# Gate and up of 256-query chunks: one copy out of PSUM and a multiplication on GpSimd, in a program ordered by a planner with other assumed step times

## The chip, the cores and the metric

The kernel runs on one core of one Trainium2 chip. The metric is the device time of one launch in microseconds (us), as the median of several runs. Five engines work side by side, each through its own list of instructions in a fixed order: TensorE (PE; PEld is its weight load), VectorE (DVE), ScalarE (ACT), GpSimd (POOL), and SyncE (SP), which here only issues DMAs. They wait for one another through semaphores. SBUF is the on-chip memory, PSUM the eight banks into which TensorE writes.

## The reference

One transformer block with 2048 tokens, width 640, 32 heads of width 20 and a bilinear feed-forward part of width 1536, all in bfloat16:

```python
mod = (silu(c) @ w_mod)                       # six vectors: sa, ca, ga, sb, cb, gb
h = layernorm(x) * (1 + ca) + sa
q, k, v = split(h @ wqkv)                     # 32 heads, 20 wide
p = softmax(q @ k.T / sqrt(20))               # 32 x 2048 x 2048
x = x + ga * ((p @ v) @ wo)
h = layernorm(x) * (1 + cb) + sb
x = x + gb * (((h @ w_gate) * (h @ w_up)) @ w_down)
```

## The kernel before

**Tiling.** The 2048 queries are cut into seven chunks, one of 512 and six of 256. For each chunk the heads are taken in eight sets of four. One pair of chunk and set is an item. TensorE writes an item's scores (L1524) into PSUM in units of 128x512, transposed, keys on the partitions (in a 256-query chunk two key tiles side by side). Then there are two ways to the exponential. ScalarE takes two units at once, 128x1024, with its own function (L1561, tile PP). Or VectorE approximates it: it adds a bias and turns the score into an int16 (L1585, tile DB, "P1"), masks it into two tiles (L1617 and L1625, tile DSS, for four units at once, a "quad"), and the first of these is multiplied with DB, on GpSimd in four pieces of 512 (L1637) or on VectorE in one piece of 2048 (L1622). The table QUADS says how many quads of each item go VectorE's way. Both kinds are multiplied with the values V on TensorE (L2192) and summed in PSUM. A quad costs TensorE two such products where a ScalarE unit costs one.

**End of an item.** VectorE transposes the sum (L1717), takes a reciprocal (L1723), GpSimd or VectorE normalizes (L1725), VectorE transposes back (L1734), and DMAs (L1746) put the rows into the tile Ocp.

**Around it.** In chunk 0 the projections of K, Q and V are still being made, spread between the scores (L1230, L970). Most of K and Q is written to DRAM (k_rows, q_rows; L1276) and read back in the layout of the scores (L1289, L1298), all issued by SP. When a chunk's heads are done, its suffix runs between the scores of the next chunk: output projection (L1827), second layernorm (L1844 to L1851), transposition (L1889), then for each of the twelve 128-wide slices of the feed-forward width a gate and an up matmul, and the down projection (tiles wd and hprod, evacuated at L2062). The last chunk's suffix stands alone at the end of the program, the tail.

**Gate and up of a 256-query chunk.** Ten groups of four matmuls fill one PSUM bank: the gate in columns 0 to 255, the up part in columns 256 to 511. Chunks 1 to 5 have twelve such rounds each, sixty in all. Then two VectorE instructions:

```python
f = lambda e: e.tensor_copy(gsb[:, gs, 0:n], ps[:, r.b["b"], 0:n])                                    # L1959
f = lambda e: e.tensor_tensor(hprod[:, fc, 0:n], ps[:, r.b["b"], n:2 * n], gsb[:, gs, 0:n], ALU.mult) # L1966
```

The tile gsb has two halves of 512 columns, used in turn, and the copy of a round waits until the product of two rounds before has been made. PSUM's bank is given back when the second instruction is done.

**What sets the order.** The kernel carries a planner. While the program is built, the class Sched steps through time with an assumed duration for each task, and at each step gives each free engine the ready task with the best priority. What comes out is a fixed list for every engine; on the chip nothing is chosen any more. Among the assumed figures: P1 and other reads of PSUM cost `n * 1.042 + 67` ns, a landing of a DMA is reckoned from its size, tasks that would share an SBUF port between VectorE and GpSimd are kept apart by a lock (LKTOL), and TensorE is fed filler matmuls (L2523) when its recent work falls below a limit (FILL_HARD, HAM_MIN). Scores come first: pick_pe issues the next pair of score units as soon as the PSUM banks for it are free, there are two sets of them, so the scores of a pair need the exponential two before to have been read. d_attach hangs a VectorE unit onto such a score group when a PSUM bank is free. Between scores TensorE gets products with V, projections and suffix rounds. The table STAGE changes some limits of the planner from item to item. The tasks touched by the change are built in `after` in `suffix`, in `packed_round`, in `item_end_tasks`, in `Sched._enable`, `Sched.finish_issue` and `d_attach`.

Of the kernel before, what the change touches and what calls it, by code (L numbers as in the profile page):

```python
# [30 lines left out]
EARLY_M = 900.0  # L31
DMA_M0 = 60000.0
# [3 lines left out]
HAM_MIN = 3100.0  # L36
# [3 lines left out]
class Task:  # L40
    __slots__ = ("head", "hval", "hknow", "eng", "dur", "lat", "deps", "emits", "ctr", "prio", "gate", "acq", "on_start", "slots",
                 "start", "done", "needed", "val", "know", "nleft", "ready", "users", "name", "mode", "seq", "rt", "sem",
                 "nbytes", "cond", "alt", "land", "firm", "lk", "dead", "key")

    def __init__(self, eng, dur, emits, deps=(), ctr=None, prio=0.0, lat=None, gate=0, acq=(), on_start=None,
# [26 lines left out]
        self.firm = False  # L72
        self.lk = 0
# [58 lines left out]
class Sched:  # L132
# [102 lines left out]
    def finish_issue(self, task, start, dur):  # L235
        task.start = start
        if task.nbytes:
# [118 lines left out]
def emit_program(nc, sched, nsem_dma=56):  # L356
# [124 lines left out]
QUADS = ((0, 4, 3, 3, 3, 4, 4, 4), (2, 2, 1, 2, 2, 2, 1, 2), (2, 2, 1, 2, 2, 2, 1, 2), (2, 2, 1, 2, 2, 2, 1, 2), (2, 2, 1, 2, 2, 2, 1, 2), (2, 2, 1, 2, 2, 2, 1, 2), (2, 1, 2, 2, 2, 1, 2, 0))  # L481
# [30 lines left out]
ZFILL = 1  # L512
WD_POOL, WD_PRIO = 1, 400.0
# [31 lines left out]
FILL_HARD = 3600.0  # L545
# [23 lines left out]
    0: {"PVMIN": 2, "HOLD": 95, "PVTOL": 249, "D_RES": 58, "PVCAP": 6, "X_HALF": 0.0, "XDPRIO": 1.343, "FILL_MIN": 3463.3, "LKTOL": 300.0, "EAGER": 9, "PVMAX": 14, "X_LATE": -179.96, "TPRIO": 0.75, "STEAL_GAP": 200, "D_LATE": 16, "PV_KEEP": 2},  # L569
    1: {"PVCAP": 15, "XBACK": 1, "FILL_MIN": 4629.7},  # L570
    2: {"DL": 0.376},
    4: {"HOLD": 58.0, "X_LATE": -39.3},
    5: {"D_LATE": 7, "PVMAX": 3},
    6: {"X_LATE": 168.4, "FILL_MIN": 5225.9, "HOLD": 156.4},
    7: {"DL": 0.501},
    8: {"FILL_MIN": 2868.8},
    10: {"X_HALF": 69.3, "HOLD": 73.7, "PVMAX": 5},
    11: {"DL": 0.443},
    12: {"DL": 0.459, "HOLD": 108.3, "X_LATE": 6.6},
    13: {"DL": 0.417},  # L580
    15: {"X_LATE": 86.8},
    16: {"HOLD": 135.0, "FILL_MIN": 4362.5},
    17: {"X_LATE": -17.4, "LKTOL": 338.9, "HOLD": 52.0},
    19: {"DL": 0.471, "PVMAX": 7, "HOLD": 113.6},
    20: {"DL": 0.391, "PVMAX": 10},
    21: {"X_LATE": -85.4, "PVMIN": 3},
    24: {"DL": 0.464, "STEAL_GAP": 210.6, "X_LATE": -52.5, "PVCAP": 14, "HOLD": 116.4, "LKTOL": 98.1},
    25: {"DL": 0.549, "LKTOL": 370.4, "HOLD": 156.3},
    26: {"DL": 0.411, "PVMIN": 1, "X_LATE": 2.0, "EAGER": 6, "X_HALF": 58.0},
    27: {"DL": 0.473},  # L590
    29: {"HOLD": 148.6, "D_LATE": 5, "LKTOL": 267.5, "D_RES": 36, "PVMAX": 3},
    30: {"EAGER": 11},
    31: {"X_LATE": -99.6, "HOLD": 173.2, "X_HALF": 164.9, "PV_KEEP": 2},
    33: {"DL": 0.442, "PVMIN": 7, "PV_KEEP": 3, "X_HALF": 147.4},
    34: {"PVMIN": 3, "X_HALF": 26.9, "STEAL_GAP": 91.8, "EAGER": 8, "X_LATE": 136.8, "D_RES": 25},
    35: {"X_HALF": 148.7},
    36: {"DL": 0.524},
    37: {"FILL_MIN": 4112.0, "EAGER": 8, "X_LATE": -201.5},
    39: {"STEAL_GAP": 162.9, "EAGER": 9},
    42: {"PVMAX": 8, "FILL_MIN": 4334.4, "PV_KEEP": 3},  # L600
    43: {"HOLD": 127.6},
    46: {"D_LATE": 20, "PV_KEEP": 3, "X_LATE": -80.9},
    53: {"LKTOL": 820.1, "X_HALF": 73.5},
    54: {"PVTOL": 279.6, "FILL_MIN": 4011.5, "X_HALF": 31.3},
# [15 lines left out]
def build_kernel(nc, A_x, A_wqkv, A_wo, B_x, B_w_gate, B_w_up, B_w_down, c, w_mod, out):  # L620
# [603 lines left out]
    def packed_round(kind, b, tc, prio, gate=0, late_q=False):  # L1224
# [69 lines left out]
        else:  # L1294
# [6 lines left out]
            if tc not in LATEQ:  # L1301
                proj_early.append(r.last)
# [1048 lines left out]
    def d_attach(ts, t, pos, rows, limit, relax):  # L2351
        n = 0
        while n < limit:
# [15 lines left out]
            if ga is None or ga[0] > t:  # L2369
                break  # L2370
# [258 lines left out]
```

## Time and profile before

| what | value |
|---|---|
| median of 3 runs | 805.0 us (804.37 to 805.67) |
| the profiled execution's own time | 805.59 us |
| its span from first to last instruction | 803.8 us |
| mean granted TensorE clock | 0.998 |
| PE busy | 790.4 us, 98% |
| ACT busy | 764.8 us, 95% |
| DVE busy | 697.8 us, 87% |
| POOL busy | 386.0 us, 48% |

The profile is of one execution. A row of a group of instructions gives the line, the engine, the operation, what it writes and reads, partitions x elements, the count, then the busy time in us, the mean time of one in ns, and after the second bar the idle time of the engine just before them with what ended it. Instructions of one engine overlap a little at their ends, so the mean of one is longer than the step from one start to the next. TensorE's busy time is modelled: a busy PE isn't a PE at its peak.

### The profile page before, as it was taken

How to read it: one execution, taken by the hardware profiler on the slowest of the kernel's cores; microseconds unless marked ns; L12 is line 12 of the kernel's file. 1: busy time of each engine (PE TensorE's matmuls, PEld its weight loads, DVE VectorE, ACT ScalarE, POOL GpSimd, SP SyncE). 2: the span in 40 equal slices, each digit the busy share in tenths (PEclk: the TensorE clock that was granted, in tenths of full speed). 3: DMA queues.
4: the chain of work that ended last, by engine and by line, in shares of the span. 5: the costliest groups of instructions: out<-in, count | busy, mean ns of one | idle time of the engine just before them, and what ended most of it. 6: DMA issues, size and time to landing. Idle time of an engine off the chain costs nothing.

```text
span 803.8 us, 37761 instructions
## 1 busy us (share of the span) xinstructions
PE 790.4 (98%) x16595; PEld 380.6 (47%) x16595; DVE 697.8 (87%) x1401; ACT 764.8 (95%) x847; POOL 386.0 (48%) x396
## 2 busy tenths in 40 slices
PE   8999999999999999999999999999999999999998
PEld 4433433333244434445555455555555555555567
DVE  7978788799989999988999999999899988898754
ACT  6899899999999999999999999999999999999961
POOL 3347455654366565763444443545534554455300
PEclk9999999999999999999999999999999999999999
DMA  9733212212341532120032404231540254414420
GB/s 297 243 113 91 62 43 64 61 33 76 92 109 50 167 88 52 35 55 13 24 81 65 95 16 112 57 73 39 121 89 15 54 118 94 98 37 106 92 68 18
DMA packets 154314, 64.66 MB, mean 80 GB/s; under 512 B 116951, under 2 KB 154151, under 8 KB 154151
## 3 DMA queue, kind: packets, MB, share of 16 engines
q1 hardware_dynamic: 153223, 61.10, 30.0%
q8 instruction: 132, 2.16, 1.1%
q10 hardware_dynamic: 928, 1.15, 0.5%
q14 instruction: 31, 0.25, 0.1%
HBM read 50.63 MB, written 8.99 MB: 74 GB/s over the span
## 4 chain that ended last, share of the span: by engine, by line
PE 77%; ACT 14%; DVE 5%; issue 2%; DMA 1%; SPq 1%; POOL 0%; DVEq 0%; ACTq 0%
PE ps_all L1524 26%; PE ps_all L970 21%; PE ps_all L2192 19%; ACT PP L1561 14%; PE ps_all L1230 4%; PE ps_all L966 3%; DVE DB L1585 2%; PE ps_all L1889 1%; PE ps_all L1166 1%; PE ps_all L1127 1%; DVE DSS L1617 1%; PE ps_all L2523 0%; DVE DSS L1625 0%; DMA QT<-q_rows 0%; PE ps_all L991 0%
## 5 line engine op out<-in xcount | busy, mean ns | idle before, releaser
L1561 ACT ACTIVATE PP<-ps_all 128x1024 bf16<-128x1024 f32 x810 | 748.5, 1090 | 6.7 <-PE ps_all L1524 4.8
L1637 POOL TENSOR_TENSOR DSS<-DB,DSS 128x512 bf16<-128x512 bf16 x268 | 305.0, 1157 | 290.6 <-DVE DSS L1625 254.2
L1585 DVE TENSOR_SCALAR DB<-ps_all 128x512 int16<-128x512 f32 x428 | 285.5, 681 | 50.5 <-PE ps_all L1524 48.0
L1524 PE MATMUL ps_all<-QT,KT 32*128 32x256 bf16 (+2 forms) x3648 | 319.4, 287 | 4.5 <-DMA QT<-q_rows 0.8
L1524 PEld LDWEIGHTS ps_all<-QT,KT 32*128 32x128 bf16 x3648 | 93.9, 92 | 204.1 <-ACT PP L1561 141.5
L2192 PE MATMUL ps_all<-PP,Vf 128*32 128x256 bf16 (+2 forms) x2892 | 163.6, 291 | 0.5 <-DVE KPB L1242 0.3
L970 PE MATMUL ps_all<-h2T,stg 128*32 128x256 bf16 (+2 forms) x2716 | 122.9, 281 | 0.3 <-DVE DB L1585 0.2
L2192 PEld LDWEIGHTS ps_all<-PP,Vf 128*32 128x32 bf16 (+1 forms) x2892 | 54.5, 94 | 76.4 <-issue 67.6
L2192 PE MATMUL ps_all<-DSS,Vf 128*32 128x256 bf16 (+1 forms) x1512 | 88.7, 291 | 0.0
L1617 DVE TENSOR_SCALAR DSS<-DB 128x2048 int16<-128x2048 int16 x107 | 77.2, 722 | 0.8
L970 PEld LDWEIGHTS ps_all<-h2T,stg 128*32 128x32 bf16 x2716 | 61.6, 96 | 26.9 <-issue 22.0
L1625 DVE TENSOR_SCALAR DSS<-DB 128x2048 int16<-128x2048 int16 x107 | 73.2, 684 | 0.8 <-PE ps_all L2192 0.8
L970 PE MATMUL ps_all<-wd,hprod 128*32 128x320 bf16 (+1 forms) x1404 | 61.0, 277 | 0.0
L1725 POOL TENSOR_TENSOR OTn<-OT,invT 128x256 bf16<-128x256 f32 (+1 forms) x49 | 35.3, 721 | 37.7 <-DVE invT L1723 37.5
L1622 DVE TENSOR_TENSOR DSS<-DB,DSS 128x2048 bf16<-128x2048 bf16 x40 | 51.5, 1287 | 0.0
L2192 PEld LDWEIGHTS ps_all<-DSS,Vf 128*32 128x32 bf16 x1512 | 36.5, 95 | 20.9 <-issue 12.4
L970 PE MATMUL ps_all<-wV,hT 128*32 128x160 bf16 x1280 | 38.9, 236 | 0.9 <-DVE DB L1585 0.3
L970 PEld LDWEIGHTS ps_all<-wd,hprod 128*32 128x32 bf16 x1404 | 31.2, 96 | 14.2 <-issue 10.8
L1717 DVE STREAM_TRANSPOSE OT<-ps_all 128x256 f32<-128x256 f32 (+2 forms) x57 | 27.1, 475 | 8.8 <-PE ps_all L2192 8.5
L1230 PE MATMUL ps_all<-hT,wk 128*32 128x512 bf16 x360 | 32.3, 382 | 0.0
L970 PEld LDWEIGHTS ps_all<-wV,hT 128*32 128x32 bf16 x1280 | 24.6, 97 | 15.9 <-issue 8.2
L1230 PE MATMUL ps_all<-hT,wq 128*32 128x512 bf16 x375 | 31.3, 382 | 0.6 <-DVE OT L1717 0.6
(133 smaller groups left out, 556.1 us busy)
## 6 DMA issues: line engine op xcount, KB each, us to landing
stg<-in_B_w_gate_dram SPq DMA_DIRECT2D x74, 160.0 KB
stg<-in_B_w_up_dram SPq DMA_DIRECT2D x74, 160.0 KB
KT<-k_rows SPq DMA_DIRECT2D x112, 32.0 KB
QT<-q_rows SPq DMA_DIRECT2D x48, 64.0 KB
Ocp<-OcT SPq DMA_DIRECT2D x164, 10.0 KB
wm<-in_w_mod_dram SPq DMA_DIRECT2D x3, 800.0 KB
x<-in_A_x_dram SPq DMA_DIRECT2D x7, 320.0 KB
k_rows<-KPA SPq DMA_DIRECT2D x16, 128.0 KB
```

What stands on the lines that cost most here:

```text
L970: return lambda e, b: e.matmul(ps[32 * x:32 * x + 32, b, c0 + o:c0 + o + w], lhs()[:, 32 * x:32 * x + 32], rhs() if w == n else rhs()[:, o ...
L1230: f = [lambda e, b_, k=k, x=x: e.matmul(ps[x:x + min(32, w - x), b_, :], wx[:, k, r0 + x:r0 + min(x + 32, w)], hT[tc][:, k, :], tile_posit ...
L1524: ems.append(lambda e, i=i, kt=kt: e.matmul(dstf()[:, i * u.n:(i + 1) * u.n], KT[32 * u.s:32 * u.s + 32, u.j, kt * 128:(kt + 1) * 128], QT ...
L1561: return e.activation(PPs[g % 2][:, cellp["p"], 0:nu * 512], ps[:, b0:b0 + nu, :].rearrange("p b c -> p (b c)"), AFT.Exp, scale=ESCALE)
L1585: return e.tensor_scalar(DBl[st_["slot"]][:, x * 512:(x + 1) * 512], bank(cell["b"]), EBIAS, 0.0, op0=ALU.add, op1=ALU.max)
L1617: return e.tensor_scalar(DSl[st_["ss"][0]][:, :], DBl[st_["slot"]][:, :], 0x7F, 0x3F00, op0=ALU.bitwise_and, op1=ALU.bitwise_or)
L1622: return e.tensor_tensor(d, DBl[st_["slot"]][:, :].bitcast(BF16), d, ALU.mult)
L1625: return e.tensor_scalar(DSl[st_["ss"][1]][:, :], DBl[st_["slot"]][:, :], 0x7F80, 2, op0=ALU.bitwise_and, op1=ALU.bitwise_or)
L1637: return e.tensor_tensor(d, DBl[st_["slot"]][:, x * w:x * w + w].bitcast(BF16), d, ALU.mult)
L1717: t1 = Task("dve", n * 1.1 + 70, lambda e: e.transpose(OT[:, 0:n], ps[:, item_info[it]["bank"], 0:n].rearrange("p (b q r) -> p b r q", q=3 ...
L1725: f3 = lambda e: e.tensor_tensor(OTn[:, 0:n].rearrange("p (b c r) -> p b r c", c=32, r=2), OT[:, 0:n].rearrange("p (b r c) -> p b r c", c= ...
L2192: ems.append(lambda e, i=i, kt=kt, stt=stt, stp=stp: e.matmul(ps[32 * s:32 * s + mc, bk, 0:u.n], Vf[:, (kt * H + 4 * u.j + s) * VW:(kt * H ...
```

## The change

For the sixty rounds of gate and up of chunks 1 to 5, one VectorE copy takes all 512 columns out of PSUM, and GpSimd multiplies the two halves within SBUF. The bank is given back by the copy; the half of gsb by the product. Beside it the planner gets other figures, and the table STAGE is another one.

```diff
+                    if GU_POOL and not tail:
+                        f = lambda e: e.tensor_copy(gsb[:, gs, 0:2 * n], ps[:, r.b["b"], 0:2 * n])
+                        fa = lambda e: e.copy(gsb[:, gs, 0:2 * n], ps[:, r.b["b"], 0:2 * n])
+                        f2 = lambda e: e.tensor_tensor(hprod[:, fc, 0:n], gsb[:, gs, n:2 * n], gsb[:, gs, 0:n], ALU.mult)
+                        eg = evac(2 * n, ps_cost(2 * n), f, fa, ds)
+                        r.hp = pool(n * POOL_NS + 180.0, f2, [eg] + (hp_free if alt else bd.get("hp", []) + proj_early + kv_last),
+                                    prio=GU_PRIO)
+                        r.hp.lk = 2
+                        return [eg]
...
-                g_use[gs] = r.evac[1]
-                hp.append(r.evac[1])
+                hpt = r.hp if GU_POOL and not tail else r.evac[1]
+                g_use[gs] = hpt
+                hp.append(hpt)
```

The planner's figures: writes of late Q rows land 900 ns later than assumed so far (QW_M), reads of Q rows 1500 ns later (QR_M); P1 starts 28 ns later after its scores (P1_X); a VectorE unit is hung onto scores only where the PSUM bank was given back by VectorE 110 ns earlier (SD_X); transposes, reciprocal and one evacuation of VectorE get other durations; two limits for filler go up; one quad fewer in chunk 1.

```diff
+QW_M, QR_M = 900.0, 1500.0
+P1_X, SD_X = 28.0, 110.0
-HAM_MIN = 3100.0
+HAM_MIN = 3150.0
...
-            t = max(t, d.done + SEM)
+            t = max(t, d.done + SEM + (P1_X if task.name[:2] == "P1" and d.mode == "S" else 0.0))
...
+            task.done += task.xm
...
-QUADS = ((0, 4, 3, 3, 3, 4, 4, 4), (2, 2, 1, 2, 2, 2, 1, 2), (2, 2, 1, 2, 2, 2, 1, 2), (2, 2, 1, 2, 2, 2, 1, 2), (2, 2, 1, 2, 2, 2, 1, 2), (2, 2, 1, 2, 2, 2, 1, 2), (2, 1, 2, 2, 2, 1, 2, 0))
+QUADS = ((0, 4, 3, 3, 3, 4, 4, 4), (1, 2, 1, 2, 2, 2, 1, 2), (2, 2, 1, 2, 2, 2, 1, 2), (2, 2, 1, 2, 2, 2, 1, 2), (2, 2, 1, 2, 2, 2, 1, 2), (2, 2, 1, 2, 2, 2, 1, 2), (2, 1, 2, 2, 2, 1, 2, 0))
...
-FILL_HARD = 3600.0
+FILL_HARD = 3700.0
...
+            if late_q:
+                t.xm = QW_M
...
+                        qt_ready[(j, ci)][0].xm = QR_M
...
-        t1 = Task("dve", n * 1.1 + 70, lambda e: e.transpose(
+        t1 = Task("dve", n * 1.1 + 84, lambda e: e.transpose(
...
-        t2 = dve(155, lambda e: e.reciprocal(invT[:, 0:nb32].unsqueeze(2),
+        t2 = dve(80 + n * .14, lambda e: e.reciprocal(invT[:, 0:nb32].unsqueeze(2),
...
-        t4 = dve(n * .55 + 65, lambda e: e.transpose(OcT[:, cell["s"], 0:n].bitcast(F32), OTn[:, 0:n].bitcast(F32)), [t3],
+        t4 = dve(n * .55 + 84, lambda e: e.transpose(OcT[:, cell["s"], 0:n].bitcast(F32), OTn[:, 0:n].bitcast(F32)), [t3],
...
+            if any(r.eng == "dve" and r.done + SEM + SD_X > t for r in G.free[ga[1]][1]):
+                break
```

More of the change, by code (lines that the diff above doesn't have):

```diff
@@ L72, in __init__ @@
         self.firm = False
+        self.xm = 0.0
         self.lk = 0
@@ L512 @@
 ZFILL = 1
+GU_POOL, GU_PRIO = 1, 1.0
 WD_POOL, WD_PRIO = 1, 400.0
@@ L596 @@
[L596 to L604 removed]
+    0: {"HOLD": 95, "D_RES": 74, "PV_KEEP": 1, "STEAL_GAP": 200, "PVMAX": 14, "XDPRIO": 1.343, "PVTOL": 249, "PVMIN": 2, "FILL_MIN": 4190.746, "X_HALF": 0.0, "PVCAP": 12, "TPRIO": 0.75, "X_LATE": -102.4, "EAGER": 9, "XBACK": 0, "LKTOL": 300.0, "D_LATE": 16},
@@ new lines @@
+    1: {"FILL_MIN": 5124.6, "XBACK": 0},
+    2: {"DL": 0.376, "EAGER": 1, "PV_KEEP": 1, "X_HALF": 49.4, "PVCAP": 9, "FILL_MIN": 4415.7, "PVMIN": 3},
+    3: {"XBACK": 1, "LKTOL": 531.1},
+    4: {"EAGER": 8},
+    6: {"FILL_MIN": 4116.5, "LKTOL": 394.8},
+    7: {"DL": 0.501},
+    8: {"X_LATE": -77.9},
+    9: {"FILL_MIN": 3350.9, "STEAL_GAP": 245.0, "HOLD": 46.2},
+    10: {"FILL_MIN": 4535.1},
+    11: {"DL": 0.443, "X_LATE": -58.4},
+    12: {"DL": 0.459, "X_HALF": 20.5},
+    13: {"DL": 0.417, "HOLD": 122.9, "STEAL_GAP": 231.9},
@@ new lines @@
+    15: {"X_LATE": 18.9, "EAGER": 12, "X_HALF": 79.9},
+    16: {"HOLD": 138.0, "XBACK": 1},
+    17: {"D_LATE": 21, "X_HALF": -32.9},
+    18: {"LKTOL": 56.8, "PVMIN": 1, "X_LATE": 10.1},
+    19: {"DL": 0.471},
+    20: {"DL": 0.391, "PVTOL": 422.6, "D_LATE": 19},
+    21: {"PVTOL": 288.1},
+    22: {"PVMAX": 7, "HOLD": 130.5, "D_RES": 16},
+    24: {"DL": 0.464, "X_LATE": 109.8},
+    25: {"DL": 0.549, "FILL_MIN": 4626.8, "PV_KEEP": 1, "PVMAX": 8},
+    26: {"DL": 0.411, "HOLD": 138.4},
+    27: {"DL": 0.473},
@@ new lines @@
+    28: {"EAGER": 7, "PVTOL": 206.9, "HOLD": 129.1},
+    30: {"X_HALF": 98.9},
+    32: {"LKTOL": 117.6},
+    33: {"DL": 0.442},
+    34: {"PV_KEEP": 3, "STEAL_GAP": 236.2},
+    35: {"HOLD": 85.7},
+    36: {"DL": 0.524},
+    38: {"HOLD": 100.7, "STEAL_GAP": 240.7, "PV_KEEP": 2},
+    39: {"LKTOL": 471.8},
+    40: {"X_HALF": 40.4, "PVTOL": 130.7, "D_RES": 9},
+    41: {"EAGER": 11, "PVMAX": 4},
+    45: {"STEAL_GAP": 187.6, "EAGER": 11},
+    46: {"X_LATE": 101.6},
+    47: {"D_LATE": 17, "X_LATE": -63.7, "HOLD": 123.0},
@@ L605 @@
+    48: {"PVCAP": 11, "X_LATE": -48.4, "HOLD": 165.9},
+    50: {"LKTOL": 277.0, "X_HALF": 20.6, "D_RES": 35},
+    56: {"HOLD": 198.9},
 }
@@ L1878, in after @@
                             else:
-                                evs.append(dve(128 * .78 + 95, lambda e, k=k: e.tensor_scalar(
+                                evs.append(dve(252, lambda e, k=k: e.tensor_scalar(
                                     h2T[:, k, sl], bankh(r.b["b"])[:, k * 128:(k + 1) * 128], mcol[:, 3, k:k + 1],
@@ L1897, in after @@
                                             bias=mcol[:, 2, k:k + 1], scale=mcol[:, 3, k:k + 1])
-                return [evac(n, n * .78 + 55, f, fa, [r.last, r_sb.evac[0], r_cb.evac[0]] +
+                return [evac(n, n * .52 + 187, f, fa, [r.last, r_sb.evac[0], r_cb.evac[0]] +
                              (first if alt else bd.get("h2T", []) + kv_last))]
```

27 lines of the change are left out of this document (1 added, 26 removed).

## The prediction

> **What bounds the kernel now.** I read the page's busy times first, then the costliest groups, the table by stretches, the waits, the chain of waits and the tail's timeline.
>
> ```profile
> PE 790.4 (98%) x16595; PEld 380.6 (47%) x16595; DVE 697.8 (87%) x1401; ACT 764.8 (95%) x847; POOL 386.0 (48%) x396
> ...
> L1561 ACT ACTIVATE PP<-ps_all 128x1024 bf16<-128x1024 f32 x810 | 748.5, 1090 | 6.7 <-PE ps_all L1524 4.8
> L1637 POOL TENSOR_TENSOR DSS<-DB,DSS 128x512 bf16<-128x512 bf16 x268 | 305.0, 1157 | 290.6 <-DVE DSS L1625 254.2
> ```
>
> Two engines look full. The exponentials tell which one is: 810 of them, and ScalarE idles 6.7 us before them in total. Read one by one in the timeline, they start 904 ns apart in more than half of the cases and never closer. The first starts at 16.35 us, the last at 774.69. 809 steps of 0.904 are 731.3 us; the rest of the 758.3 us, **27.0 us, is lateness**. After the last start come 29.1 us of tail. So span = 16.35 + 731.3 + 27.0 + 29.1 = 803.8, and a change can win only in the lateness, the number of exponentials, and the tail.
>
> ```profile
> 80.00:120.00 40.00, 38.67 (x667) 14.90 (x663) 30.73 (x59) 36.62 (x40) 20.29 (x18) 0.96 0.19 52
> 200.00:240.00 40.00, 39.05 (x656) 13.76 (x649) 37.56 (x65) 39.67 (x43) 20.91 (x21) 1.00 0.37 100
> 480.00:520.00 40.00, 39.91 (x1025) 21.85 (x1020) 37.31 (x77) 39.97 (x44) 18.50 (x19) 1.00 0.37 85
> ```
>
> The columns are the stretch, its length, then busy time of PE, PEld, DVE, ACT, POOL, the granted clock, and DMA. From 120 us on ScalarE is busy 39.7 to 40.0 of 40; only 80 to 120 has a hole. By starts, the lateness is 5.8 us before 40 us, 1.5 to 86, 4.55 from 86 to 106 (18 steps), 0.3 to 120, and 14.9 from 120 on (707 steps, 0.021 each).
>
> ```profile
> PEld ps_all L1524 <- ACT PP L1561: 117.3, 416, 0.8
> ...
> PEld ps_all L970 <- DVE DB L1585: 5.0, 18, 0.4
> ...
> PEld ps_all L2192 <- DVE DB L1585: 4.6, 20, 0.4
> ```
>
> These waits are of 120 to 765 us: who waits for what, total, times, longest. 416 score groups wait for ScalarE (0.28 us on average), so TensorE has some slack but little; when it stands behind VectorE's P1 (DB), the next scores can be late. Of the 14.9 us, 68 exponentials more than 60 ns late carry 9.6. In the 2.2 us before them TensorE had waited for VectorE or GpSimd in cases worth 5.9 us (half of it for DB), and for neither in 3.7.
>
> ```profile
> 86.33 1.24 SPq L1289
> ...
> 89.88 0.72 SPq L1746
> ...
> 90.71 3.51 DMA QT<-q_rows
> ```
>
> This is the chain of waits: SP gets through a K read and four moves of finished rows before it can issue a read of Q rows, which lands 3.51 us later; scores wait for it.
>
> **The change, part by part.** Counts are from the two built programs' lists of instructions.
>
> *Gate and up.* Sixty copies of 128x256 (412 ns, L1959) and sixty products (413 to 414 ns, L1966) go from VectorE, 49.5 us; sixty copies of 128x512 come. The nearest rows, 128x512 casts out of PSUM, have 674 (L1986) and 686 ns (L1239): 40.6 us. VectorE gains 8.9. One quad fewer takes off 4 x 0.681 + 0.722 + 0.684 = 4.1; four more products L1622 on VectorE cost 4 x 1.287 = 5.1, three more copies in the tail 1.3. Net **6.6 us less VectorE**, 1% of 697.8, thickest in the stretches of the sixty rounds.
>
> GpSimd's new product, 128x256 within SBUF, is in no row. Rows of the same kind have 1157 ns for 512 columns and 1401 for 640 (L1503), a slope of 1.91 ns: 0.67 us for 256; the 256-column row of another input type (L1725) says 665. I bound it by 0.4 (VectorE's time) and 1.16. 60 x 0.67 = 40 us, less 20 pieces L1637 (23 us): POOL goes from 386 to 403 us, half of the span, which hides it. A copy stands in VectorE's queue until the product two rounds before is done, with P1 and the masks behind it and the scores behind those. In the new list the rounds are mostly four exponentials apart, so two rounds give some 7 us; a product behind one piece needs 1.16 + 0.67. I cost this wait at nothing, with the port as a rival below.
>
> *ScalarE.* 812 exponentials for 810, otherwise the same list: 2 x 0.904 = **+1.8 us**, all on the path.
>
> *The tail.* This is the dearest part. After the last score TensorE has 511 matmuls, before it had 409: chunk 5's down projection (hprodt) leaves 144 instead of 48, the output projection 24 instead of 18.
>
> ```profile
> 778.42 0.59 PE L970 MATMUL ps_all<-wd,hprodt 128*32 128x320 bf16 x12
> 778.94 0.45 PE L1867 MATMUL ps_all<-ident,xn2c 128*128 128x128 bf16 x5
> 779.32 1.27 PE L970 MATMUL ps_all<-wd,hprodt 128*32 128x320 bf16 x32
> 780.73 2.91 PE L966 MATMUL ps_all<-h2Tc,stx 128*128 128x128 bf16 x49
> ```
>
> TensorE's starts (us, length, line, count). Four hprodt matmuls run side by side, and such a pass follows the last after 136 ns: 24 passes are 3.3 us, six output matmuls of 136 ns 0.8. From 774.4 to 801.1 TensorE is busy without a hole: the down projection that it has already covers the layernorm chain up to 780.73, so none of the new work finds an empty place. **+4.1 us.** What it leaves was done before the last score, where ScalarE runs at 40.00 of 40 and gives nothing back. Bounds: 3.3 if the output matmuls fit elsewhere, 4.1.
>
> *The hole at 86 to 106 us.* Its loss of 4.55 us less the ordinary 18 x 0.021 leaves 4.2 to win at most, 0 at least (the same queue of moves stands ahead of the read in the new list). The scores that wait for this read are now the 73rd group, the round that makes these rows ends at the 59th; before, 72nd and 60th. That is two steps, 1.8 us, more room; TensorE waited 0.82 us for the read. I also add up TensorE's work between each two scores: 109 ns for a pass of 256 columns, 215 for a score group, 95 for each turn between scores and other work (a score start to the next product start is 198 ns). The filled gap ahead of that read was 1.98 us, now two of 1.29 and 1.34: 0.25 less over the step. The exponentials after it (96.7, 99.5, 104.6 us) are 1.8 us late, behind P1 steps that wait for the same read; I take 1.3 of it. Sum 0.8 + 0.25 + 1.3 = **-2.35**. The half clock that follows this hole (0.96 in its row, so 1.7 us of clock lost) touches exponentials only 0.3 us late: **-0.2**.
>
> *From 120 us on.* Gaps too full for one step add up to 2.1 us of excess before and 1.3 after: -0.8. Waits for VectorE: the new figures for P1 and for banks fresh from VectorE aim at the larger half of the 5.9, and VectorE has 1% less to do. No row shows what a new order leaves. I bound the gain by 5.9 (all gone) and by -3.4 (the port, below), and take half, -3.0: the larger half is aimed at, while other waits are drawn anew. Together **-3.8**.
>
> *Sum* on the profiled execution's 805.59 us (1.8 us lie around its span): 805.59 + 1.8 + 4.1 - 2.35 - 0.2 - 3.8 = 805.1. It stands 0.6 above the median of the runs shown, so I forecast **804.5**.
>
> **Rivals.** About 0.2%, 1.6 us, is what a measurement of this kernel can tell from no change.
>
> *The order fits the chip much better.* All 5.9 us of waits for VectorE go and the hole closes: savings 4.2 + 0.2 + 5.9 + 0.8 = 11.1 against costs of 5.9: 799.8. For it: half of the waits are those that the figures aim at. Against it: a new order has its own waits. Chance 0.33.
>
> *The down projection in the tail is paid and the middle gives nothing back: slower.* Savings are 2.55 alone: 805.0 + 5.9 - 2.55 = 808.3. It decides as soon as savings fall below 4.3 us. For it: the tail's 4.1 us are counted, in a stretch without holes, and the middle already runs 0.925 us per exponential. Against it: 9.6 us are in few, large latenesses. Chance 0.19.
>
> *GpSimd's product holds up VectorE.* Masks L1617 take 683 ns in the median and up to 1481, L1622 1214 and up to 1797, the long ones beside a POOL instruction: 26, 7 and 22 overlapped ones of L1617, L1625 and L1622 average 173, 63 and 136 ns over the others, 7.9 us in all. If every second new product stops such a step for half its 0.67 us, that is 10 us, more than the 6.6 saved; VectorE idles only 2 to 3 us of 40 there. The surplus of 3.4 us then falls on the scores: 808.3 + 3.4 = 811.7. It decides from some 6.6 us on. Chance 0.08, as the old pieces rarely do it.
>
> The Trainium skill (SBUF — State Buffer, Who interferes with whom) speaks against this change: a VectorE step in a two-port mode or with two SBUF inputs, and a GpSimd step that reads SBUF, shut each other out for a whole instruction, while a VectorE step with one SBUF input, as the old product was, doesn't. The long masks here agree; the page has no count of such meetings, and the sum doesn't use it.
>
> **How the numbers follow.** My forecast has the remaining 0.40, of which 0.05 falls under 803.4 and 0.02 above 806.6. Faster 0.33 + 0.05 = 0.38, slower 0.19 + 0.08 + 0.02 = 0.29, same 0.33. The range goes from the first rival's 799.8 to 809.5, above the second and short of the third; the likeliest case's own is 802.5 to 806.5.
>
> **What would show it.** Right: 812 exponentials with the first at 16.35 us; 33.2 us from the last start to the end; the lateness from 86 to 106 near 2 us and that from 120 near 11; products near 0.67 us. Wrong: a tail of 29 us, long masks beside hprod, VectorE idle behind a copy, or another late read in place of this one.

## The result, and the profile after

The changed kernel took **807.65 us** (median of 6 runs, 807.10 to 811.08), the kernel before 804.47 in 6 runs (802.95 to 805.67): a ratio of 1.0042, 95% interval 1.0022 to 1.0062. It is slower, by 3.2 us, where I had forecast no measurable change. (The ratios here and below are those on record; they can differ from the quotient of the two medians by up to 0.0014.)

The page of the changed kernel: busy times, and the groups that the change and the forecast touch (line, instruction, tiles, count; busy us, mean ns; idle time before them).

```profile
PE 793.5 (98%) x16607; PEld 380.3 (47%) x16607; DVE 693.8 (86%) x1342; ACT 763.2 (95%) x846; POOL 400.2 (50%) x436
...
L1575 ACT ACTIVATE PP<-ps_all 128x1024 bf16<-128x1024 f32 x812 | 747.9, 1119 | 5.0 <-PE ps_all L1538 3.4
L1651 POOL TENSOR_TENSOR DSS<-DB,DSS 128x512 bf16<-128x512 bf16 x248 | 282.5, 1157 | 252.7 <-DVE DSS L1639 224.7
...
L1979 POOL TENSOR_TENSOR hprod<-gsb 128x256 bf16<-128x256 bf16 x48 | 32.1, 671 | 34.9 <-DVE DSS L1639 11.3
L1977 DVE CAST gsb<-ps_all 128x512 bf16<-128x512 f32 x60 | 40.6, 678 | 9.7 <-PE ps_all L981 9.7
```

The instructions came at their forecast prices: product 671 ns, copy 678. VectorE's busy time fell by 4.0 us, not 6.6. The forecast added up mean durations, and these fell by 8.7 us; but instructions overlap at their ends, and VectorE now has 59 fewer: before, 1401 durations of 785.4 us in sum made 697.8 us of busy time, 63 ns of overlap for each. ScalarE still sets the pace; it does two steps more.

The table by stretches, same columns as before:

```profile
80.00:120.00 40.00, 39.74 (x696) 14.89 (x692) 31.71 (x63) 38.55 (x43) 23.52 (x21) 1.00 0.20 54
200.00:240.00 40.00, 39.05 (x684) 14.70 (x680) 36.20 (x67) 39.34 (x43) 13.60 (x16) 1.00 0.37 96
480.00:520.00 40.00, 39.86 (x1000) 21.32 (x998) 37.37 (x66) 40.00 (x45) 18.13 (x21) 1.00 0.36 85
```

The hole of 80 to 120 us is smaller (ScalarE 38.55 for 36.62) and without a half clock. The stretch from 200 lost a little (39.34 for 39.67).

The waits from 120 to 765 us (who waits for what; total, times, longest):

```profile
PEld ps_all L1538 <- ACT PP L1575: 131.3, 491, 0.7
...
PEld ps_all L2216 <- DVE DB L1599: 4.9, 23, 0.2
...
PEld ps_all L981 <- DVE DB L1599: 4.5, 17, 0.4
```

The two waits for VectorE's P1 that the new figures aim at were 4.6 and 5.0 us; they are 4.9 and 4.5. The chain of waits, which ran through SP and the read of Q rows between 86 and 94 us, now runs through TensorE and ScalarE there.

The tail's timeline (start, length, engine, line, count); the last exponential starts at 772.29:

```profile
778.36 0.45 PE L1881 MATMUL ps_all<-ident,xn2c 128*128 128x128 bf16 x5
778.74 2.77 PE L981 MATMUL ps_all<-wd,hprodt 128*32 128x320 bf16 x76
781.44 0.45 PE L1881 MATMUL ps_all<-ident,xn2c 128*128 128x128 bf16 x5
781.82 1.14 PE L981 MATMUL ps_all<-wd,hprodt 128*32 128x320 bf16 x28
782.89 3.30 PE L977 MATMUL ps_all<-h2Tc,stx 128*128 128x128 bf16 x56
```

The gate and up of the last chunk (h2Tc) starts 10.6 us after the last exponential's start; before, 6.04 us. The same sum as in the prediction, for the profiled executions:

| us | before | after | forecast of after |
|---|---|---|---|
| first exponential's start | 16.35 | 16.33 | 16.35 |
| steps of 0.904 | 731.3 (809) | 733.1 (811) | 733.1 |
| lateness | 27.0 | 22.8 | 20.65 |
| of it 40 to 86 us | 1.5 | 1.85 | 1.5 |
| of it 86 to 106 us | 4.55 | 2.27 | 2.2 |
| of it from 120 us | 14.9 | 12.8 | 11.1 |
| tail from the last start | 29.1 | 33.4 | 33.2 |
| span | 803.8 | 805.7 | |
| the execution's time | 805.59 | 807.46 | |
| median | 804.47 | 807.65 | 804.5 |

(The forecast lateness is 27.0 less 2.35, 0.2 and 3.8.) Costs: 1.8 + 4.3 us. Gains: 4.2 us against the profiled execution of before, which stands 1.1 above its median.

### The profile page after: what moved, and what is told of

It reads as the page before. It is cut to its first block, busy times and chain, and to the rows that moved or that the text cites. A ratio compares the mean times of both kernels' runs of the same rounds, so it can differ in the third digit from the quotient of the medians.

```text
span 805.7 us, 37809 instructions
## 1 busy us (share of the span) xinstructions
PE 793.5 (98%) x16607; PEld 380.3 (47%) x16607; DVE 693.8 (86%) x1342; ACT 763.2 (95%) x846; POOL 400.2 (50%) x436
## 4 chain that ended last, share of the span: by engine, by line
PE 58%; ACT 32%; issue 5%; DVE 4%; DMA 1%; SPq 0%; ACTq 0%; DVEq 0%
ACT PP L1575 32%; PE ps_all L1538 19%; PE ps_all L981 15%; PE ps_all L2216 13%; PE ps_all L1241 4%; PE ps_all L977 3%; DVE DB L1599 2%; PE ps_all L1177 1%; DMA wm<-in_w_mod_dram 1%; PE ps_all L1138 1%; PE ps_all L2549 1%; DVE DSS L1639 1%; PE ps_all L1903 1%; DVE DSS L1631 0%; PE ps_all L1002 0%
## 5 line engine op out<-in xcount | busy, mean ns | idle before, releaser
L1651 POOL TENSOR_TENSOR DSS<-DB,DSS 128x512 bf16<-128x512 bf16 x248 | 282.5, 1157 | 252.7 <-DVE DSS L1639 224.7
L1599 DVE TENSOR_SCALAR DB<-ps_all 128x512 int16<-128x512 f32 x424 | 282.4, 681 | 51.5 <-PE ps_all L1538 49.3
L2216 PE MATMUL ps_all<-PP,Vf 128*32 128x256 bf16 (+3 forms) x2900 | 164.6, 291 | 0.3 <-DVE Vf L1333 0.3
L981 PE MATMUL ps_all<-h2T,stg 128*32 128x256 bf16 (+2 forms) x2788 | 126.1, 278 | 0.7 <-DVE xckb L2086 0.4
L1639 DVE TENSOR_SCALAR DSS<-DB 128x2048 int16<-128x2048 int16 x106 | 73.7, 695 | 0.0
L1636 DVE TENSOR_TENSOR DSS<-DB,DSS 128x2048 bf16<-128x2048 bf16 x44 | 55.7, 1269 | 0.1
L1979 POOL TENSOR_TENSOR hprod<-gsb 128x256 bf16<-128x256 bf16 x48 | 32.1, 671 | 34.9 <-DVE DSS L1639 11.3
L1977 DVE CAST gsb<-ps_all 128x512 bf16<-128x512 f32 x60 | 40.6, 678 | 9.7 <-PE ps_all L981 9.7
L1241 PE MATMUL ps_all<-hT,wk 128*32 128x512 bf16 (+1 forms) x360 | 32.6, 382 | 0.0
```

What stands on the lines that cost most here:

```text
L981: return lambda e, b: e.matmul(ps[32 * x:32 * x + 32, b, c0 + o:c0 + o + w], lhs()[:, 32 * x:32 * x + 32], rhs() if w == n else rhs()[:, o ...
L1241: f = [lambda e, b_, k=k, x=x: e.matmul(ps[x:x + min(32, w - x), b_, :], wx[:, k, r0 + x:r0 + min(x + 32, w)], hT[tc][:, k, :], tile_posit ...
L1599: return e.tensor_scalar(DBl[st_["slot"]][:, x * 512:(x + 1) * 512], bank(cell["b"]), EBIAS, 0.0, op0=ALU.add, op1=ALU.max)
L1636: return e.tensor_tensor(d, DBl[st_["slot"]][:, :].bitcast(BF16), d, ALU.mult)
L1639: return e.tensor_scalar(DSl[st_["ss"][1]][:, :], DBl[st_["slot"]][:, :], 0x7F80, 2, op0=ALU.bitwise_and, op1=ALU.bitwise_or)
L1651: return e.tensor_tensor(d, DBl[st_["slot"]][:, x * w:x * w + w].bitcast(BF16), d, ALU.mult)
```

## The experiments

Every time is a median; each ratio is to the kernel before, measured beside it (medians of 804.25 to 804.78 us). Lateness and tail are of one profiled execution each, with the step of 0.904 us; profiles of the changed kernel's list differ by some 0.3 us in lateness. "List kept" means that the order of the changed kernel, or of the kernel before, was made first and the edit put into it, so that nothing else moves.

My theory after the result: the two exponentials and the deferred down projection cost 6.1 us; the new instructions by themselves are worth 2 us; the rest of the lateness is waits. Rivals: GpSimd's product gets in VectorE's way; and TensorE is so full that what is taken from the tail comes back ahead of it.

### The tail

**Two thirds of the tail's deferred passes left out, list kept** (e1).

```diff
+    late_ = [t for t in pe_[ls_ + 1:] if t.name[:3] == "dn5"]
...
+        if 2 <= pos_[id(t)] % FT <= 9:
+            out_.add(id(t))
...
+    sc.all = [t for t in sc.all if id(t) not in out_]
```

> The changed kernel with its order frozen; 24 of the 36 passes of the last query chunk but one's down projection that stand after the last score are left out (16 of 24 in two of its rounds' middles), so those output rows lack terms. If the tail is a sum of TensorE's work, 24 x 0.136 = 3.3 us go: tail 30.1 us, ratio to before about 1.000. Rival: the second tile's transposes wait for its layernorm chain, which ends at 781.3 us with or without the passes ahead of it, and the gate and up matmuls stand behind them; then only the seven passes behind the transposes count, 1.0 us: tail 32.4, ratio about 1.003. If the GpSimd products are what costs, neither. Lateness from 120 us on stays at 12.8 us in all cases.

808.57 us, 1.0044 [1.0024, 1.0063]; lateness 23.0, tail 34.2 us: 0.8 more with 96 matmuls less. Neither expectation held. TensorE's timeline there (in brackets: idle time before, and what ended it), and the stretches (first column after the lengths: PE; the clock follows POOL):

```profile
778.54 0.45 PE L1881 MATMUL ps_all<-ident,xn2c 128*128 128x128 bf16 x5 [1.14 <-DVE xn2c L1865]
778.92 1.00 PE L981 MATMUL ps_all<-wd,hprodt 128*32 128x320 bf16 x24
781.57 0.72 PE L1881 MATMUL ps_all<-ident,xn2c 128*128 128x128 bf16 x5 [1.65 <-DVE xn2c L1865]
```

```profile
776.00:781.00 5.00, 2.73 (x43) 1.26 (x41) 4.74 (x18) 0.00 (x0) 1.06 (x2) 1.00 0.00 0
781.00:785.00 4.00, 3.43 (x39) 2.50 (x40) 2.19 (x6) 0.81 (x2) 0.04 (x1) 0.57 0.15 51
```

The order of the list still puts the second transposes ahead of gate and up, and these wait for the layernorm. So the passes had covered that wait, and without them the clock went to half for 3.4 us, over the second transposes and the start of gate and up. The Trainium skill (TensorE: Matmul & The Clock Gate, Why this matters for your kernels) asks for no gaps over about 3 us between matmuls; here the clock fell after two shorter gaps, of 1.14 and 1.65 us, 2.8 us of the 4.2 up to 781.57.

**The same passes left out before the order is made** (e5), so that the planner can place gate and up anew; up to the last score the lists are the same.

```diff
-                for fc in range(FT):
+                for fc in (0, 1, FT - 2, FT - 1) if ci == NC - 2 and (tl, c_) != (0, 0) else range(FT):
```

> As e1, 24 passes of that down projection left out, but left out before the order is made: the lists are the changed kernel's until after the last score, and from there gate and up of the last chunk's first tile stand ahead of the second tile's transposes, as in the kernel before. Both theories of the tail expect the chain of the first tile to set the start of gate and up, about 2.7 us earlier: tail 30.6, ratio to before about 1.001. If the tail isn't what costs, no change.

805.31 us, 0.9996 [0.9978, 1.0014]; tail 30.9, lateness 23.1. Without the deferred work the tail is 2.46 us shorter. In this order gate and up of the first tile stand ahead of the second transposes; TensorE idles 1.1 us before them:

```profile
780.38 1.90 PE L977 MATMUL ps_all<-h2Tc,stx 128*128 128x128 bf16 x31 [1.13 <-DVE h2Tc L1893]
```

This run has the 48 matmuls of the kernel before behind its last score, and still its tail is 1.8 us longer than 29.1: gate and up start 7.9 us after the last exponential's start in place of 6.04, and TensorE waits for VectorE's part of the layernorm there. In the count, the 24 output matmuls in place of 18 are what is left as a difference; they weren't tried alone.

**All of the work done, with the last stages ordered otherwise** (e8): other values for the planner's stages from the 46th item on.

```diff
-    46: {"X_LATE": 101.6},
+    46: {"X_LATE": 101.6, "X_HALF": 123.8, "LKTOL": 582.1, "D_LATE": 6, "STEAL_GAP": 201.2, "D_RES": 50, "PV_KEEP": 2, "PVTOL": 150.1, "XBACK": 0, "EAGER": 9, "PVCAP": 14, "DL": 0.418, "HOLD": 136.0},
...
```

> The changed kernel, with other figures for the stages from the 46th item on, so that only the last part of the order differs: after the last score stand 104 matmuls of the last down projection (26 passes of four) in place of 144, 24 of the output projection as before; 812 exponentials. Theory (the deferred work's price is its place behind the last score): the tail falls by ten passes of 0.136 us, from 33.4 us to 32.0, and the time to some 806.3. Rival (TensorE is as full before the last score as after it, so what moves forward delays scores by as much): tail 32.0, lateness up by 1.4 us, 807.7 as the changed kernel.

805.62 us, 1.0007 [0.9991, 1.0022]: 2.0 us below the changed kernel. Lateness 22.82, as before the edit; tail 30.98. The rival falls: ten passes moved ahead of the last score and made nothing late. The tail gave 2.4 us, not 1.36, for a second reason that its timeline shows:

```profile
777.31 3.04 PE L987 MATMUL ps_all<-wd,hprodt 128*32 128x320 bf16 x84
780.28 2.29 PE L983 MATMUL ps_all<-h2Tc,stx 128*128 128x128 bf16 x38
782.45 0.45 PE L1887 MATMUL ps_all<-ident,xn2c 128*128 128x128 bf16 x5
```

Fewer turns between kinds of work, five of the passes half as wide, the last score 0.27 us earlier before its exponential, and gate and up started 7.9 us after the last start in place of 10.6, ahead of the second transposes. So 2.4 of the 4.3 us that the tail cost, 2.0 in the time, are a matter of the order of its end, not of the change's instructions.

### The instructions in the new order

**VectorE's old two instructions, list kept** (e3); GpSimd keeps a 32-column step in the product's place.

```diff
+                        eg.emits = [lambda e: e.tensor_copy(gsb[:, gs, 0:n], ps[:, r.b["b"], 0:n])]
+                        r.hp.emits = [lambda e: e.tensor_tensor(gsb[:, gs, n:n + 32], gsb[:, gs, 0:32], gsb[:, gs, 0:32], ALU.mult)]
+        tt_ = Task("dve", eg_.dur, f_, [eg_] + own_, name="hpair")
```

> The changed kernel with its order frozen, but each of the sixty rounds has the old pair of VectorE instructions in the place of the one copy; GpSimd keeps a 32-column product that nobody uses, for its place in the order. VectorE gets 60 x (412 + 413 - 678) = 8.8 us more, GpSimd some 30 us less. If the instruction change itself is worth what VectorE gains, lateness from 120 us on rises by 1.5 to 4 us, ratio to before 1.006 to 1.009. If it is worth nothing, since scores don't wait for VectorE there, ratio 1.003 to 1.005. If GpSimd's products cost more than they save, it falls below 1.003.

810.04 us, 1.0057 [1.0038, 1.0076]; lateness 24.9, 2.1 more, most of it from 440 to 600 us; tail as it was. In this order the new instructions are 2.4 us better than the old.

**A fill in place of the product, list kept** (e2): GpSimd writes 0.5 into hprod (312 ns) instead of multiplying.

```diff
-f2 = lambda e: e.tensor_tensor(hprod[:, fc, 0:n], gsb[:, gs, n:2 * n], gsb[:, gs, 0:n], ALU.mult)
+f2 = lambda e: e.memset(hprod[:, fc, 0:n], 0.5)
```

> The changed kernel with its order frozen; GpSimd fills the 256 columns of the product with a constant instead of multiplying (no multiplication, nothing read from SBUF), the waits stay. If the product neither makes anyone wait nor shuts VectorE out, the time stays within 0.7 us of the changed kernel's, ratio to before 1.003 to 1.005, and the masks beside GpSimd keep their lengths. Rival (the shared port or a late product costs): sixty products shorter by some 0.4 us and without reads give back 1 to 3 us, ratio 1.000 to 1.003, lateness from 120 us on down by as much.

807.87 us, 1.0030 [1.0013, 1.0046]; lateness 22.15. The product costs nothing that can be measured. Up to here my theory stood: the pair is worth 2 us, the order loses 6.

### The instructions in the old order

**The kernel before, list kept, with the new pair** (e6). Each copy of 128x256 becomes one of 128x512, each product goes to GpSimd at its place; banks are given back by the copy.

```diff
+        eg_.emits = [f_ if eg_.eng == "dve" else fa_]
+        t_ = Task("pool", 670.0, f2_, [eg_] + list(hq_.deps), name="hq")
```

> The order of the kernel before is kept, and only the sixty gate and up rounds change their instructions: one VectorE copy of 128x512 in the place of the copy of 128x256, and GpSimd's product in the place of VectorE's product. ScalarE's and TensorE's lists are those of before: 810 exponentials, 48 matmuls of the last down projection after the last score. Theory (the instructions are worth 2 us wherever they stand, the rest of the change is two exponentials and the deferred down projection): lateness falls from 27.0 us to some 25, the tail stays at 29.1, the time is 802.1 to 803.5, a ratio of 0.997 to 0.999. Rival (the 2 us that the old pair lost in the new order were lost because that order was made without it): the old order was made without these products too, so they meet masks and OTn steps and hold up the copy two rounds later: lateness 27 to 30 us, 804.5 to 808.

**819.45 us**, 1.0181 [1.0156, 1.0206]; lateness 39.6, tail 30.8. The theory fell: the instructions aren't worth 2 us wherever they stand; here they cost 15. VectorE's busy time is 701.9 us, *more* than before, though each round has one instruction fewer. One meeting with a normal product (VectorE's own product of 2048 columns, L1622 in the kernel before), from the timelines of VectorE and GpSimd:

```profile
531.51 1.21 DVE L1624 TENSOR_TENSOR DSS<-DB,DSS 128x2048 bf16<-128x2048 bf16 x1
```

```profile
531.58 1.67 POOL L1973 TENSOR_TENSOR hprod<-gsb 128x256 bf16<-128x256 bf16 x1
```

The product was held beside the normal product and ended 0.53 us after it, 1.67 us in all in place of 0.67. 31 times a mask or normal product lay beside a product; 19 products took from 1.05 to 1.67 us. What masks and normal products take over their usual time (680 and 1212 ns), where it is more than 40 ns, adds up to 16.6 us, 8.0 in the kernel before; I call this the lengthening. At the end the down projection waits 2.4 us for a product in GpSimd's queue, and TensorE's clock is at half for 10.2 us from 763.4 on:

```profile
764.02 0.73 PE L972 MATMUL ps_all<-wd,hprodt 128*32 128x320 bf16 x8 [2.40 <-POOL hprodt L1973]
```

Between 765 and 775 us, behind this one wait, the exponentials lose 6.2 us; the whole lateness grew by 12.6. So about half of the loss is a wait for GpSimd's queue and the half clock after it, not the sum of the meetings.

**The same with the fill** (e11).

```diff
-    lambda e: e.tensor_tensor(hprod[:, fc, 0:n], gsb[:, gs, n:2 * n], gsb[:, gs, 0:n], ALU.mult)
+    lambda e: e.memset(hprod[:, fc, 0:n], 0.5)
```

> The order of the kernel before with one copy of 128x512 on VectorE, as in the run that kept the old order and took 819 us; but GpSimd fills the product's place with a constant (128x256 of hprod, 312 ns, nothing read) instead of multiplying, so the terms of the gated branch are left out. Theory (the products meet VectorE's masks: in that run 31 masks lay beside a product, masks and normal products together were lengthened by 16.6 us, 7.9 in the kernel before, and 19 products took up to 1.67 us instead of 0.67): without a step that reads the memory both engines read, the masks lose 8 us again and the time comes back to 803 to 806, lateness 25 to 28 us. Rival (the loss is that the copy and the down projection now wait for a second engine's queue): the queue is the same and only 0.36 us shorter per step, 19 steps of up to 1.67 us become 0.31; most of the loss stays: 812 or more.

808.91 us, 1.0049 [1.0030, 1.0067]; lengthening 8.6 us, lateness 31.1. 10.5 of the 15 us are gone, 4 are left: between the two expectations, nearer to the first. The fill is both shorter and without reads, and TensorE no longer waits 2.4 us at the end, so this run doesn't tell the meetings' share from the queue's. It doesn't end all meetings either. Beside the same normal product as above the fill took its usual 0.31 us, as nine others beside normal products did; but the three that started while VectorE ran a mask of 0.68 us were held, 0.79 us each:

```profile
532.58 0.31 POOL L1973 MEMSET hprod<- 128x256 bf16 x1
```

```profile
495.26 0.79 POOL L1973 MEMSET hprod<- 128x256 bf16 x1 [0.26 <-DVE gsb L1971]
```

**The real product, put behind masks** (e12): 26 products wait for one to five VectorE steps more.

```diff
+            if not vl_[q + 1].lk and (vl_[q + 1].dur > 640 or not vl_[q + 2].lk):
+                if q > p_:
+                    t_.deps = t_.deps + [vl_[q]]
```

> The order of the kernel before, one copy of 128x512 on VectorE and the real product on GpSimd; but where a mask or normal product stands within the next VectorE steps, the product waits until VectorE has two steps ahead of it that are none (26 of the 60 are put behind one to five VectorE steps). If meeting masks is what cost 14 us in the old order: products of 0.67 us again, masks near 8 us of lengthening, 805 to 810. If waiting for GpSimd's queue is what cost: the products end later still, 819 or more.

819.44 us, 1.0185 [1.0161, 1.0208]. Only 7 times does a mask or normal product lie beside a product, and two products take over 0.7 us, but the lengthening is still 16.4 us: 11.5 of it lies beside the GpSimd pieces (L1639 there) that now run later, 5.9 with the fill. So the meetings moved to GpSimd's next step. The time is also the one that the second expectation gave (819 or more), and TensorE waits for products here too: 1.65 us before 678.6 and 2.4 us before 767.8, each with a half clock of 3.4 us after it; behind these two waits the exponentials lose 6.6 us. That left open whether the changed kernel escapes by its waits or by its places.

### The waits in the new order

In the changed kernel 49 of the 60 products carry a wait for the mask or normal product planned ahead of them (lk = 2 in the diff). What the products wait for:

```profile
L1979 POOL TENSOR_TENSOR hprod<-gsb x48: 665/672/677, 406.4 to 690.2; 128x256 bf16<-128x256 bf16 x48
...
  DVE DSS L1639: 11.3, 6
  DVE DSS L1636: 10.5, 8
  DVE DSS L1631: 7.0, 7
  DVE gsb L1977: 6.1, 5
```

After min/median/max of the product come the idle times of GpSimd ahead of it: 28.8 of 34.9 us end with a mask or normal product, and no product takes over 677 ns.

**The changed kernel, list kept, without these 49 waits** (e16).

```diff
+    for t, m in sc.held:
+        if any(t is x for x in gup):
+            own = [d for d in t.deps if d is not m or False]
+            t.deps = own
```

> The changed kernel with its lists unchanged on every engine, but 49 of the 60 GpSimd products no longer wait for the VectorE mask or normal product planned ahead of them; they start as soon as their copy is done and GpSimd reaches them. No data hangs on these waits. Theory (the products cost nothing in the new order because the waits keep them off the masks): some 20 to 30 products beside a mask in place of 6, products of up to 1.7 us again, masks and normal products lengthened by 12 to 17 us in place of 7.6, lateness 25 to 30 us, 810 to 815. Rival (the places in the new order alone keep them apart, or the meetings in the old order only hurt because other steps there were late): 10 meetings or fewer, 807 to 808.5.

810.30 us, 1.0074 [1.0058, 1.0089]: 2.7 us slower. 33 meetings in place of 6, lengthening 11.5 us, a little less than I expected. The product's line:

```profile
L1983 POOL TENSOR_TENSOR hprod<-gsb x48: 662/671/1667, 408.8 to 695.1; 128x256 bf16<-128x256 bf16 x48
```

From 440 to 600 us lateness is 4.5 us in place of 2.3. (It is also 2.1 more from 200 to 280 us, where no product runs: this execution has a half clock there, which is not the edit's.) So the waits keep the products clear, not the places alone; and the new order can pay for them, as e12's old order couldn't.

The Trainium skill (SBUF — State Buffer, Who interferes with whom), cited in the prediction, describes what is seen beside the 1.67 us: the one that comes second stands still until the first is done.

**One meeting cleared** (e14): the GpSimd normalisation (OTn) that starts at 198.81 us waits for the mask that it met. That mask in VectorE's timeline of the changed kernel:

```profile
199.19 1.53 DVE L1639 TENSOR_SCALAR DSS<-DB 128x2048 int16<-128x2048 int16 x1
```

```diff
+    otn_.deps = otn_.deps + [ex_]
```

> The changed kernel, with one wait more: the GpSimd normalisation (OTn) that started at 198.81 us, beside a VectorE mask that took 1531 ns, starts after that mask. If the meeting made the score at 200.9 us late by 0.65: that mask takes 0.68 us, no exponential near 200.9 us is late by more than 0.1, total lateness 22.2 in place of 22.8, 807.0. Rival (the score was late for another wait beside it): lateness as before, 807.6.

807.15 us, 1.0024 [1.0011, 1.0037]. Lateness 22.14, the expected 0.67 less. VectorE's timeline of this run:

```profile
199.17 0.68 DVE L1639 TENSOR_SCALAR DSS<-DB 128x2048 int16<-128x2048 int16 x1
```

and no exponential is late at 200.9 us any more.

**All planned meetings made binding** (e15).

```diff
+            m_ = [x for x in masks_ if x.done <= t.start + 100.0 and at_[id(x)] < at_[id(t)]]
+            t.deps = t.deps + m_[-1:]
...
+        m_ = [x for x in pl_ if x.start + x.dur <= t.start + 1.0 and at_[id(x)] < at_[id(t)]]
+        t.deps = t.deps + m_[-1:]
```

> The changed kernel, with its planned order of the masks and normal products on VectorE and GpSimd's steps made binding: each of these GpSimd steps waits for the last such VectorE step planned before it, and the other way round. Nothing else is moved. If meetings that the order didn't foresee are what the rest of the lateness comes from: the lengthening of 7.6 us goes to under 1, and lateness falls by 1 to 3 us, 805 to 807. Rival (the waits stop VectorE as long as the meetings did, and what comes late somewhere is handed on): lateness as before or 1 to 4 us more, 807.6 to 812.

808.29 us, 1.0048 [1.0030, 1.0066]. No mask is lengthened at all, VectorE is busy 689.4 us, 4.4 less, and lateness is 23.7, 0.9 more. The rival held: taken together, the masks that wait made the exponentials no less late than the masks that were stopped. Whether the other 6.7 us of lengthening cost lateness by themselves this run can't tell, since each is traded for a wait; waits on both sides don't win them back.

### Versions

**The kernel before with other values for its last stages** (e9).

```diff
-    43: {"HOLD": 127.6},
+    43: {"HOLD": 147.6, "PVMIN": 4, "D_LATE": 8, "D_RES": 35, "PVTOL": 239.9, "XBACK": 0, "STEAL_GAP": 102.2, "PVCAP": 5},
...
```

> The kernel before, with other figures for the stages from the 40th item on: 810 exponentials, 48 matmuls of the last down projection after the last score as before, 16 of the output projection in place of 18. Theory (number of exponentials and tail carry the time, an order drawn anew changes the lateness by little): tail 28.8 us, 804.0, ratio 0.998 to 1.001. Rival (each new order of the middle has its own late reads and waits, and the old one happened to be good): lateness from 600 us on up by over 2 us, 806 or more.

**803.40 us**, 0.9986 [0.9975, 0.9998]: the best of all, below both kernels by a little. Lateness 25.9, tail 28.7. Its row of the hole:

```profile
80.00:120.00 40.00, 39.49 (x699) 15.14 (x700) 31.70 (x62) 38.49 (x42) 20.26 (x18) 1.00 0.19 53
```

The list up to here is that of the kernel before, and yet ScalarE is busy 38.49 us, not 36.62, at the full clock. I come back to this.

**Both: the order of e9, and in it the new pair as in e6** (e10).

```diff
+        t_ = Task("pool", 670.0, f2_, [eg_] + list(hq_.deps), name="hq")
```

> Both edits at once: the kernel before with the other figures for its last stages, and in that order the sixty rounds with one copy of 128x512 on VectorE and the product on GpSimd. If the instructions are worth 2 us wherever they stand: 2 us below the run with the figures alone, some 802, lateness 24 to 25 us. If they pay only in an order made for them: as the run with the figures alone, or up to 4 us above it.

812.96 us, 1.0098 [1.0070, 1.0126], 9.6 above e9, over twice what I gave as the worst; lengthening 15.8 us (25 of 255 masks and normal products were over their time in e9, 41 here). Of the 8.4 us of added lateness, 4.0 lie between 759 and 765 us, behind a wait of TensorE of 1.5 us for one of GpSimd's pieces and a half clock of 6.8 us. A second order that wasn't made for the products pays for them too.

**The changed kernel with the end of e8 and the wait of e14** (e17).

```diff
+    otn_.deps = otn_.deps + [ex_]
```

> Both edits that helped the changed kernel at once: the other figures for its last stages (104 matmuls of the last down projection after the last score) and the one wait that keeps the normalisation at 198.8 us off a mask. If the two gains, 2.0 and 0.5 us, are independent: lateness 22.1, tail 31.0, 805.1. If the last score's lateness is handed on differently in the other order of the end: 805.6, as the first edit alone.

805.02 us, 1.0010 [0.9998, 1.0023]; lateness 22.0, tail 31.0. The two gains add up: 2.6 of the 3.2 us that the change lost are back. The two exponentials, 1.8 us, stay.

## Why the prediction was wrong, point by point

- **The two exponentials** (+1.8): right.
- **The tail** (+4.1): right in size, 4.3, but by luck. The sum was 3.3 for 24 passes and 0.8 for six output matmuls; with the passes gone (e5) the tail is only 2.46 shorter, and 1.8 stay, at a wait for the layernorm. That none of the new work finds an empty place was wrong: e1 shows that some of the passes covered such a wait, and e8 that over half of the cost was order.
- **The hole at 86 to 106 us** (-2.35): the changed kernel has the forecast 2.27 us there, but most of the gain was not the change's. Five more executions with the list of before up to 106 us have 3.12 (e6), 2.26 (e9), 2.27 (e10), 3.68 (e11) and 2.27 us (e12); the profiled one had 4.55, and it alone a half clock there. All ten profiles of the changed kernel's list have 2.27 to 2.29. So the old order is late there in some executions and the new one in none; against the old order's middle value, 2.7, the gain is 0.4, and against three of its executions it is nothing.
- **From 120 us on** (-3.8): this failed. The profile shows -2.1. The step "take half, -3.0: the larger half is aimed at" has no support: the two waits for P1 went from 9.6 to 9.4 us. In e3, which has the new order with VectorE's old two instructions, lateness from 120 us on is 14.7, as good as the 14.9 of the kernel before. So what the middle gave back came with the instruction pair, for which the sum has no term of its own; for the planner's figures by themselves no gain is shown. (The order was made for the new pair, so e3 is no clean test of them.)
- **The step to the median** (-0.6): this was counted twice. The profiled execution's hole was 1.85 us over the middle value, and the execution stood 1.1 us above the median: as far as the runs tell, this is the same loss. I took the hole's gain off that execution and then also the distance to the median.
- The sum of what failed: 1.7 from 120 us on, 0.6 counted twice, 0.35 more lateness at 40 to 86 us that I hadn't looked at, 0.25 in the tail; 2.9 of the 3.15 us between forecast and result. The rest is the after execution's 0.2 below its median.
- **VectorE's 6.6 us less** came as 4.0, since the overlaps of the 59 instructions weren't reckoned with. Such time has no fixed price: e3 gives VectorE 8.5 us more and is 2.4 us slower, e15 takes off another 4.4 us and is no faster.
- **The rivals.** The second (tail paid, middle gives nothing back, 808.3) came nearest, though the middle did give back 2 us. The third (the port) had the wrong place: in the changed kernel 6 meetings, in the old order 31 and 15 us. I had read the wait behind the masks (lk = 2) in the diff as none of the costs; it is what makes the change possible, for 2.7 us (e16).

## What stays open

The old order's loss of 15 us is of two kinds, meetings and TensorE's waits for GpSimd's queue with a half clock behind them. The second carries about half of the lateness in e6, e10 and e12, but meetings make the queue late as well, and no run separates the two. e11 leaves 4 us without any product that reads; where they come from stays open. Which part of the 2.4 us of e3 is the instructions and which the order made for them can't be separated: list and pair were made for each other. How the planner's single figures (P1_X, SD_X, QW_M, QR_M) share in the middle's gain wasn't tried one by one.

## What to carry to other kernels

Before a saving is taken off a profiled execution, ask how that stretch looks in other executions of the same list: a hole with a half clock in it may be this execution's own, and its gain must not be counted against the median. In an ordered kernel an instruction has no price of its own: the same pair was worth +2.4 us in the order made for it and -15 in another; a step moved to an engine with a shared port needs its place and its wait with it. A saving of an engine's time is best added up from its busy time, not from mean durations that overlap. Work put into a full tail is paid there, but look first at what it covers: take it out without moving what waits behind it, and the tail may get longer.

## What the runs showed of the hardware

- A GpSimd product of 671 ns beside a VectorE normal product of 1.21 us took 1.67 us, and a mask beside a GpSimd step up to 1.53 us in place of 0.68. A GpSimd fill of the same 128x256 took its 0.31 us beside a normal product (ten times in e11), but 0.79 us where it started while a mask of 0.68 us was running (three times); the lengthening with it is 8.6 us, 8.0 in the kernel before.
- TensorE's clock went to half for 3.4 us after two gaps of 1.14 and 1.65 us within 4.2 us (e1), and for 10.2 us after one of 2.4 us (e6). Between 60 us and the end of TensorE's work it fell seven times in the profiles shown here, and in the 3.4 us ahead of each fall TensorE had been busy for 1.0 to 2.35 us. No single gap tells: in the kernel before the longest was 0.82 us, while one of 1.36 us in e11 passed without a fall.
- The same list had from 2.26 to 4.55 us of lateness in one stretch of 20 us, from execution to execution; another list had the same value to 0.02 us in ten.
